# Decay attention into two mixture layers on one core: first weight halves loaded ahead of the third unit, mixture steps ordered behind earlier scores

## The chip, the cores and the metric

One core of one Trainium2 chip runs the whole program in one launch. The metric is device time in microseconds (us), start to end of the launch. The median of three runs before the change is 562.1 us (561.58 to 562.75).

## The reference

Three stages follow each other; each reads what the one before it wrote.

```python
# 1. attention with decay, b over blocks of 64 positions, 2 batches x 8 heads, head size 64
intra = (q_b k_b^T * Dmask) v_b
inter = (q_b * lam**(pos+1)) kv_state
out_b = intra + inter
kv_state = lam**block * kv_state + (k_b * lam**(block-1-pos))^T v_b
# 2. first mixture layer on the 1536 x 512 rows
h = x @ w_in            # 512 x 2048, given as 64-bit floats
x2 = (h * cos(h)) @ w_out
# 3. second mixture layer: each row goes to one of 8 experts
e = argmax(x2 @ w_gate)
y = relu(x2[e] @ w1[e]) @ w2[e] * softmax_weight * sigmoid(x2 @ w_output_gate)[e]
```

## The kernel before

**Attention** is cut into 12 units u0 to u11 of 128 positions (6 chunks x 2 batches, the batches in turn). A unit has three parts, and the loop over `i` at the end of the program issues part 1 of unit i, part 2 of unit i-1 and part 3 of unit i-2. Part 1 (`a_s1`) turns the keys and the queries on TensorE (tiles tkT and tqT, in two PSUM buffers), ACT copies them to SBUF as kT and qT, DVE multiplies the turned queries by powers of lambda (qw), and POOL scales the keys (kd). Part 2 (`a_s2`) makes the scores sc on TensorE, and DVE multiplies them by the decay (pt). Part 3 (`a_s3`) makes the new state sn on TensorE, in one of the same two PSUM buffers as tkT and tqT, then the output o in one PSUM buffer, from qw and the state st and from pt and the values; DVE folds sn into st; ACT and DVE split o into two parts xs (a rounded part and the rest) for the next layer.

**Weights of the first mixture layer** come as 64-bit floats, half by half (128 x 512 numbers, 512 KB). `w_load` asks for the next half on the SP queue into a buffer raw; `w_split` converts it: ACT takes the high words (x, L207), DVE does three operations on x (L208, L209, L211), ACT rounds the result into the weight tile (w_in or w_out, L219), POOL subtracts and writes the rest (L220). x has two buffers. The constant SPLITS says in which round `i` halves are converted: one in each of rounds 2 to 5, two in rounds 6 and 7. The first step needs four halves of w_in: two for each of the first two weight pieces, of which the first piece alone is needed by step 0.

**Mixture steps** B(j, p) multiply 256 rows (block j) by weight piece p: 24 matmuls h of 256 columns (L443), a cosine chain on ACT and DVE (L472 to L478), 12 matmuls acc of 512 columns (L455), which come two steps later. Six such steps (NSA) are issued inside the attention loop, one in each round from START = 6 on, the rest behind it.

**What sets the order.** The kernel is written without hand-placed waits. A scheduler takes the instructions as the program issues them and fixes an order for each engine; every engine then runs its own list strictly in that order, and semaphores between engines are put in by the framework. `tc.issue_after(ins)` makes the scheduler place every instruction of the block that runs on the engine of `ins` behind `ins`.

**The end.** `finish` scales the result of an expert's tile (ACT for the first 128 rows, DVE for the second), and an indirect DMA from POOL scatters the rows to the output.

Of the kernel before, what the change touches and what calls it, by code (L numbers as in the profile page):

```python
# [8 lines left out]
F32 = mybir.dt.float32  # L9
F32R = mybir.dt.float32r  # L10
BF16 = mybir.dt.bfloat16
I32 = mybir.dt.int32
AF = mybir.ActivationFunctionType
ALU = mybir.AluOpType
# [14 lines left out]
def kernel(  # L29
# [93 lines left out]


    HP = 2
    steps = [("B", j, p) for j in range(FIRST) for p in range(HP)]
    NSA = len(steps)
    steps += [("B", j, p) for p in range(NP) for j in range(FIRST, NB)]
# [56 lines left out]
    def w_split():  # L185
        i = nxt["split"]
        if i >= len(order):
            return
        nxt["split"] += 1
        key = order[i]  # L190
        r = raw_t.pop(key)
        if key[0] in ("w1", "w2"):
            t = w_tile(key[0] == "w1", place(*key), "w_" + "_".join(str(z) for z in key))
            nc.scalar.copy(out=t[:, 0, :], in_=r)  # L194
            nc.vector.tensor_sub(out=t[:, 1, :], in0=r, in1=t[:, 0, :].bitcast(F32))  # L195
            wt[key] = t
        else:
            name, p, f = key
            if f == 0:
                wt[name, p] = w_tile(name == "in", p, f"w_{name}_{p}")  # L200
            t = wt[name, p]
            words = r.rearrange("p (n t) -> p n t", t=2)
            low, high = words[:, :, 0], words[:, :, 1]
            x = cv_p.tile([128, ROW], I32, tag="x", name="x")[:, 0:512]


            nc.scalar.activation(out=x.bitcast(F32), in_=high.bitcast(F32), func=AF.Copy, scale=F64_SCALE)  # L207
            nc.vector.tensor_scalar(x, x, 3, None, ALU.logical_shift_left)  # L208
            nc.vector.scalar_tensor_tensor(  # L209
                out=x, in0=low, scalar=29, in1=x, op0=ALU.logical_shift_right, op1=ALU.bitwise_or)  # L210
            nc.vector.scalar_tensor_tensor(  # L211
                out=x, in0=high, scalar=-0x80000000, in1=x, op0=ALU.bitwise_and, op1=ALU.bitwise_or)
            xf = x.bitcast(F32)
            if name == "in":
                xf = xf.rearrange("p (k f) -> p k f", k=KD)
                hi, lo = [t[:, s].rearrange("p (k f) -> p k f", k=KD)[:, :, f * 128:(f + 1) * 128] for s in range(2)]
            else:
                hi, lo = [t[:, s, f * 512:(f + 1) * 512] for s in range(2)]
            nc.scalar.copy(out=hi, in_=xf)  # L219
            nc.gpsimd.tensor_sub(out=lo, in0=xf, in1=hi.bitcast(F32))  # L220
        w_load()
# [4 lines left out]
    def wB(key, s, f):  # L226
# [8 lines left out]
        tc.tile_pool(name="at2", bufs=2),  # L235
        tc.tile_pool(name="at3", bufs=3),
        tc.tile_pool(name="raw2", bufs=2),
    ]
    qk_p, v_p, at2, at3, pools["raw2"] = [c.__enter__() for c in at_cms]
    ps_cms = [  # L240
        tc.tile_pool(name="ps_tr", bufs=2, space=PSUM),
        tc.tile_pool(name="ps_sc", bufs=2, space=PSUM),
# [57 lines left out]
    def setup_late():  # L300
        nc.gpsimd.memset(ones, 1.0)
        nc.gpsimd.memset(upper, 1.0)
        nc.gpsimd.affine_select(
            out=upper, in_=upper, compare_op=ALU.is_gt, fill=0.0, base=0,
            pattern=[[1, 128]], channel_multiplier=-1)
        nc.gpsimd.memset(accoh, 0.0)
        nc.gpsimd.memset(skip, 0.0)
        nc.gpsimd.iota(lane, pattern=[[0, 1]], base=CAP, channel_multiplier=1, allow_small_or_imprecise_dtypes=True)
        for e in range(E):
            nc.gpsimd.memset(iota8[:, :, e:e + 1], float(e - E))  # L310
            nc.gpsimd.memset(eoff[:, :, e:e + 1], float(e * CAP))
        nc.gpsimd.iota(tid, pattern=[[CH, NCH], [S, B]], base=0, channel_multiplier=1)
        nc.gpsimd.memset(wgs, 0.0)
        for w, o in ((w_gate, 0), (w_og, E)):
            nc.sync.dma_start(out=wgs[:, :, o:o + E], in_=w.rearrange("(k p) e -> p k e", p=128))

# [4 lines left out]
    def xs_tile(slot, name="xs"):  # L321
        return xs_p.tile([128, 2, KD, TB], F32R, tag=f"xs{slot}", name=name)

    kT_t, qT_t, qw_t, kd_t, p_t = {}, {}, {}, {}, {}

    def turned(src, pool, name):
        ps = ps_tr.tile([128, PR, 128], F32, tag="tr", name="t" + name)
# [21 lines left out]
    def a_s2(u):  # L349
        if u < 0 or u >= NU:  # L350
            return
        kT = kT_t.pop(u)
        qb = qT_t.pop(u)
        pt = at2.tile([128, H, CH], F32, tag="pt", name="pt")

        sc = [ps_sc.tile([128, PR, CH], F32, tag="sc", name="sc") for _ in range(2)]
        for pr in range(PR):
            for t in range(2):
                to = slice(64 * t, 64 * t + 64)
                nc.tensor.matmul(sc[t][:, pr, :], lhsT=kT[to, pr, :], rhs=qb[to, pr, :], start=True, stop=True)  # L360
        for t in range(2):
            nc.vector.tensor_mul(out=pt[:, t::2, :], in0=sc[t], in1=dec[:, t::2, :])
        p_t[u] = pt

    def a_s3(u):
# [5 lines left out]
        if c + 1 < NCH:  # L371
            kd = kd_t.pop(u)
            sn = ps_tr.tile([128, PR, 64], F32, tag="tr", name="sn")
            for h in range(H):
                sl = slice(64 * (h % 2), 64 * (h % 2) + 64)
                nc.tensor.matmul(  # L376
                    sn[sl, h // 2, :], lhsT=kd[:, h, :], rhs=vs[:, h, :], start=True, stop=True)
        o = ps_o.tile([128, PR, 128], F32, tag="o", name="o")
        if c > 0:
            qw = qw_t.pop(u)  # L380
            for pr in range(PR):
# [254 lines left out]

    rows, scl = {}, {}

    def finish(acc, t, s, who):
        y = tmp_p.tile([128, DM], F32, tag="a", name="y")  # L640
        if t == 0:
            nc.scalar.activation(out=y, in_=acc, func=AF.Copy, scale=s[:, t:t + 1])  # L642
        else:
            nc.vector.tensor_scalar(y, acc, s[:, t:t + 1], None, ALU.mult)
        put = nc.gpsimd.indirect_dma_start(  # L645
            out=out, out_offset=bass.IndirectOffsetOnAxis(ap=who, axis=0),
            in_=y, in_offset=None, bounds_check=NT - 1, oob_is_err=False)
        apart(put, puts)
# [165 lines left out]
    def second(i):  # L814
# [4 lines left out]
        if ph == "B":  # L819
# [3 lines left out]
                half_evac(j, acc_t.pop(j))  # L823
            if p == NP - 1:
                r_evac(j, acc_t.pop(j))
                parts = [(r_tr, (j,), 0), (r_mm, (j,), 2), (r_arg, (j,), 1), (r_rank, (j,), 3)]
                if j == EARLY:
                    parts += [(h_rows, (0,), 0), (r_skip, (), 2)]
                if j == FIRST - 1:
                    parts.append((routed, (), 0))  # L830
                if j == EARLY:
                    w_load()
                rout.append({"since": 0, "parts": parts})
            if j == (NB if p < HP else FIRST) - 1:
                del wt["out", p]
        elif ph == "H":
# [9 lines left out]
        else:  # L846
# [10 lines left out]
            if p == EP - 1:  # L857
                acc_t.pop(j)
                s, who = scl.pop(j)
                for z in range(2):  # L860
                    finish(accs[z], z, s, who[:, z, :])

    todo = 0

# [37 lines left out]
            h_prep(1, 1)  # L902

    SPLITS = [0, 0, 1, 1, 1, 1, 2, 2]
    START = 6
    for i in range(NU + 2):
        a_load(i + 2)
        if i == 0:
            for _ in range(4):
                w_load()  # L910
        a_s1(i)
        if i == 0:
            setup_late()
        a_s2(i - 1)
        if i == 1:
            setup_powers()
# [1 line left out]
        for _ in range(SPLITS[i] if i < len(SPLITS) else 0):  # L918
            w_split()
        if START <= i < START + NSA:  # L920
            step(i - START)
        if i >= 9 and i % 2:
            b_split(FIRST + (i - 9) // 2)

    for c in reversed(at_cms):
        c.__exit__(None, None, None)
    del pools["raw2"]
    pools["att"].__exit__(None, None, None)
    seconds(NSA)
    for c in reversed(ps_cms):  # L930
# [124 lines left out]
```

## Time and profile before

| what | value |
|---|---|
| median of 3 runs | 562.1 us |
| the profiled execution | 562.26 us |
| its span, first to last instruction | 560.4 us |
| TensorE (PE) busy | 539.1 us, 96% |
| DVE, ACT, POOL busy | 339.0, 306.2, 101.5 us |
| HBM read and written | 67.31 and 18.24 MB |

The profile gives times within the span; 1.86 us of the profiled execution lie outside it. A matmul's end is modelled, so that two that follow each other overlap in the rows; the start of the next one tells what a group took. PEld is the weight load in front of a matmul. "Idle before" is the time that an engine stood still in front of an instruction, with the instruction that ended it.

### The profile page before, as it was taken

The numbers are of one execution on the slowest core, as the hardware profiler recorded it, in microseconds if no ns is written. First come the engines' busy times: TensorE is split into PE (matmuls) and PEld (weight loads), VectorE is DVE, ScalarE is ACT, GpSimd is POOL, SyncE is SP. The second block draws the span as 40 slices with busy tenths as digits, with TensorE's granted clock in tenths as the row PEclk, the third lists the DMA queues.
The fourth block names the chain that finished last, engine by engine and source line by source line (L and its number), as shares of the span: only waits on it lengthen the run. The fifth ranks groups of instructions, "written<-read, shape, count | busy, mean of one in ns | idle before, by whom it ended". The sixth has DMA issues, their size and how long they took to land.

```text
span 560.4 us, 9916 instructions
## 1 busy us (share of the span) xinstructions
PE 539.1 (96%) x3940; PEld 479.3 (86%) x3940; DVE 339.0 (60%) x604; ACT 306.2 (55%) x492; POOL 101.5 (18%) x129
## 2 busy tenths in 40 slices
PE   8699999999999999999999989999999999999993
PEld 7578888889898999988898969799999999999982
DVE  4787647587878764345564569734677764855110
ACT  3455546477776765554554597625766654643110
POOL 4443400223222230001111200211011101101011
PEclk9999999999999999999999999999999999999997
DMA  8999841044533374201262345851688975740000
GB/s 196 258 262 282 228 133 39 10 142 151 187 114 113 113 280 145 76 39 40 66 203 79 91 139 190 258 198 55 196 287 292 296 246 183 252 156 25 1 26 34
DMA packets 84296, 85.24 MB, mean 152 GB/s; under 512 B 41486, under 2 KB 66062, under 8 KB 83472
## 3 DMA queue, kind: packets, MB, share of 16 engines
q1 hardware_dynamic: 82000, 78.09, 45.4%
q0 software_dynamic: 2240, 6.42, 2.9%
q8 instruction: 33, 0.54, 0.4%
q14 instruction: 23, 0.19, 0.1%
HBM read 67.31 MB, written 18.24 MB: 153 GB/s over the span
## 4 chain that ended last, share of the span: by engine, by line
PE 57%; issue 23%; DMA 9%; DVE 4%; POOL 3%; ACT 2%; SPq 0%; POOLq 0%; DVEq 0%; ACTq 0%
PE h L443 20%; PE acc L455 20%; DMA out_dram<-y,who 4%; PE hh L712 4%; PE acc L733 2%; DMA raw<-in_moe_w_dram 2%; PE sc L360 2%; POOL out_dram L645 2%; PE o L389 2%; PE o L384 2%; DMA xs_d<-xrow,si 2%; PE tqT L329 1%; PE sn L376 1%; DVE w_w L195 1%; DMA q<-in_q_dram 1%
## 5 line engine op out<-in xcount | busy, mean ns | idle before, releaser
L455 PE MATMUL acc<-w_out,g 128*128 128x512 f32 x576 | 141.5, 394 | 0.3 <-ACT g L477 0.3
L455 PEld LDWEIGHTS acc<-w_out,g 128*128 128x128 f32 x576 | 104.8, 188 | 21.5 <-issue 1.2
L443 PE MATMUL h<-xs,w_in 128*128 128x256 f32 x720 | 93.1, 284 | 3.7 <-POOL w_in L220 2.6
L443 PEld LDWEIGHTS h<-xs,w_in 128*128 128x128 f32 x720 | 89.4, 190 | 7.4 <-POOL w_in L220 3.0
L195 DVE TENSOR_TENSOR w_w<-raw,w_w 128x1024 fp32r<-128x1024 f32 x64 | 76.9, 1222 | 25.3 <-ACT w_w L194 25.1
L194 ACT CAST w_w<-raw 128x1024 fp32r<-128x1024 f32 x64 | 65.7, 1048 | 33.4 <-DMA raw<-in_moe_w_dram 27.0
L443 PEld LDWEIGHTS h<-xs,w_w 128*128 128x128 f32 x576 | 72.0, 191 | 1.9
L443 PE MATMUL h<-xs,w_w 128*128 128x256 f32 x576 | 72.6, 282 | 0.0
L455 PE MATMUL acc<-w_w,g 128*128 128x512 f32 x288 | 69.9, 393 | 0.0
L474 DVE SCALAR_TENSOR_TENSOR a<-a,t 128x512 f32<-128x512 f32 x48 | 36.0, 750 | 46.7 <-ACT a L473 46.7
L455 PEld LDWEIGHTS acc<-w_w,g 128*128 128x128 f32 x288 | 52.6, 188 | 10.1
L443 PE MATMUL h<-xback,w_in 128*128 128x256 f32 x432 | 55.5, 283 | 0.0
L443 PEld LDWEIGHTS h<-xback,w_in 128*128 128x128 f32 x432 | 52.8, 189 | 1.7 <-issue 1.2
L472 ACT ACTIVATE t<-h,quarter 128x512 f32<-128x512 f32 x48 | 32.9, 686 | 35.4 <-PE h L443 35.2
L645 POOL DMA_INDIRECT out_dram<-y,who x16 | 19.1, 1195 | 162.4 <-ACT y L642 146.5
L477 ACT CAST g<-a 128x512 fp32r<-128x512 f32 x48 | 29.7, 619 | 28.1 <-DVE a L476 28.0
L476 DVE TENSOR_TENSOR a<-t,h 128x512 f32<-128x512 f32 x48 | 32.9, 684 | 16.9 <-ACT t L475 16.0
L475 ACT ACTIVATE t<-a 128x512 f32<-128x512 f32 x48 | 30.3, 631 | 18.5 <-DVE a L474 18.4
L478 DVE TENSOR_TENSOR g<-a,g 128x512 fp32r<-128x512 f32 x48 | 33.9, 707 | 10.1 <-ACT g L477 9.3
L473 ACT ACTIVATE a<-t,magic 128x512 f32<-128x512 f32 x48 | 34.8, 724 | 1.1
L599 POOL DMA_INDIRECT xs_d<-xrow,si x12 | 15.1, 1261 | 101.0 <-DVE si L597 73.9
L702 DVE SCALAR_TENSOR_TENSOR g<-h,g 128x512 fp32r<-128x512 f32 x24 | 16.5, 687 | 25.7 <-ACT g L701 25.6
(144 smaller groups left out, 632.4 us busy)
## 6 DMA issues: line engine op xcount, KB each, us to landing
raw<-in_moe_w_dram SPq DMA_DIRECT2D x64, 512.0 KB, 4.7
raw<-in_moe_w_in_dram SPq DMA_DIRECT2D x16, 512.0 KB, 3.9
raw<-in_moe_w_out_dram SPq DMA_DIRECT2D x16, 512.0 KB, 3.6
xs_d<-zrow SPq DMA_DIRECT2D x16, 266.0 KB, 3.9
x_d<-xrow SPq DMA_DIRECT2D x6, 532.0 KB, 2.9
rows<-xs_d SPq DMA_DIRECT2D x6, 532.0 KB, 4.5
k<-in_k_dram SPq DMA_DIRECT2D x12, 256.0 KB, 4.9
q<-in_q_dram SPq DMA_DIRECT2D x12, 256.0 KB, 4.9
```

The costliest lines, as they stand in the source:

```text
L194: nc.scalar.copy(out=t[:, 0, :], in_=r)
L195: nc.vector.tensor_sub(out=t[:, 1, :], in0=r, in1=t[:, 0, :].bitcast(F32))
L443: nc.tensor.matmul(h[:, f * n:(f + 1) * n], lhsT=wA(key, ws, kk, f), rhs=x[:, xx, kk, :], start=(z == 0), stop=(z == 3 * KD - 1))
L455: nc.tensor.matmul(accs[t], lhsT=g[:, gs, f, t * 128:(t + 1) * 128], rhs=wB(key, ws, f), start=(first and n == 0), stop=(last and n == 5))
L472: head = nc.scalar.activation(out=t, in_=h, func=AF.Identity, bias=quarter, scale=INV2PI / WIDE)
L473: heads.append((head.ins, nc.scalar.activation(out=a, in_=t, func=AF.Identity, bias=magic).ins))
L474: nc.vector.scalar_tensor_tensor(out=a, in0=a, scalar=MAGIC, in1=t, op0=ALU.subtract, op1=ALU.subtract)
L475: nc.scalar.activation(out=t, in_=a, func=AF.Sin, scale=-TWOPI)
L476: nc.vector.tensor_mul(out=a, in0=t, in1=h)
L477: nc.scalar.copy(out=g[:, 0].rearrange("p f t -> p (f t)"), in_=a)
L478: nc.vector.tensor_sub(out=g[:, 1].rearrange("p f t -> p (f t)"), in0=a, in1=g[:, 0].rearrange("p f t -> p (f t)").bitcast(F32))
L645: put = nc.gpsimd.indirect_dma_start(out=out, out_offset=bass.IndirectOffsetOnAxis(ap=who, axis=0), in_=y, in_offset=None, bounds_check=NT ...
```

## The change

Seven edits, five of them in the attention loop:

1. In round 0 two halves of w_in are asked for ahead of the loads of unit u2, and two behind it; before, all four behind it.
2. A pool cv2 of two more buffers holds x of every second half while the attention runs.
3. The outputs o of u1 and u2 go to the PSUM pool of acc; the others stay in the one buffer of ps_o.
4. The loads of the two gate matrices (16 KB each) move from round 0 to round NU = 12, the start of the end of the loop.
5. Each step in the attention loop is placed behind the last score matmul of unit i-3: step 0 behind the scores of u3.
6. In the last expert's second tile, `finish` gives half of the columns to ACT and half to DVE.
7. The routing jobs count their delay from the turn in which they are put down, with delay 1 for the first part in place of 0, except for the last of them.

```diff
-            x = cv_p.tile([128, ROW], I32, tag="x", name="x")[:, 0:512]
+            x = (pools["cv2"] if "cv2" in pools and i % 2 else cv_p).tile([128, ROW], I32, tag="x", name="x")[:, 0:512]
...
+        tc.tile_pool(name="cv2", bufs=2),
...
+    def setup_gates():
         for w, o in ((w_gate, 0), (w_og, E)):
             nc.sync.dma_start(out=wgs[:, :, o:o + E], in_=w.rearrange("(k p) e -> p k e", p=128))
...
-                nc.tensor.matmul(sc[t][:, pr, :], lhsT=kT[to, pr, :], rhs=qb[to, pr, :], start=True, stop=True)
+                scored[u] = nc.tensor.matmul(
+                    sc[t][:, pr, :], lhsT=kT[to, pr, :], rhs=qb[to, pr, :], start=True, stop=True)
...
-        o = ps_o.tile([128, PR, 128], F32, tag="o", name="o")
+        early = u + 2 < START and u % 3
+        o = (pools["acc"] if early else ps_o).tile([128, PR, 128], F32, tag="acc" if early else "o", name="o")
...
-    def finish(acc, t, s, who):
+    def finish(acc, t, s, who, last=False):
...
+        elif last:
+            half = DM // 2
+            nc.scalar.activation(out=y[:, 0:half], in_=acc[:, 0:half], func=AF.Copy, scale=s[:, t:t + 1])
+            nc.vector.tensor_scalar(y[:, half:], acc[:, half:], s[:, t:t + 1], None, ALU.mult)
...
-                parts = [(r_tr, (j,), 0), (r_mm, (j,), 2), (r_arg, (j,), 1), (r_rank, (j,), 3)]
+                parts = [(r_tr, (j,), 0 if j == FIRST - 1 else 1), (r_mm, (j,), 2), (r_arg, (j,), 1), (r_rank, (j,), 3)]
...
-                rout.append({"since": 0, "parts": parts})
+                rout.append({"since": clock[0], "parts": parts})
...
     for i in range(NU + 2):
+        if i == 0:
+            for _ in range(2):
+                w_load()
         a_load(i + 2)
         if i == 0:
-            for _ in range(4):
+            for _ in range(2):
                 w_load()
         a_s1(i)
         if i == 0:
             setup_late()
+        if i == NU:
+            setup_gates()
...
         if START <= i < START + NSA:
-            step(i - START)
+            with tc.issue_after(scored[i - 3].ins):
+                step(i - START)
```

What the scheduler makes of it, at three places. The line numbers of the change are its own: L396 was L389 (o from pt), L391 was L384 (o from qw and the state), L364 was L360 (scores), L381 was L376 (sn), L333 was L329 (turning), L450 was L443 (h).

TensorE, from the scores of u2 to those of u3, before; w_in_344 is the first weight piece, st_174 the state of the first batch:

```order
L360 MATMUL sc<-qT,kT 128x128 x8
L389 MATMUL o<-pt,v 64x128 x8
L384 MATMUL o<-qw,st_174 64x128 x8
L389 MATMUL o<-pt,v 64x128 x8
L443 MATMUL h<-xs,w_in_344 128x256 x20
L329 MATMUL tkT<-ident,k 128x128 x4
L443 MATMUL h<-xs,w_in_344 128x256 x4
L329 MATMUL tqT<-ident,q 128x128 x4
L376 MATMUL sn<-v,kd 64x64 x8
L360 MATMUL sc<-qT,kT 128x128 x8
```

TensorE, the same stretch and on to the first h, now:

```order
L364 MATMUL sc<-qT,kT 128x128 x8
L391 MATMUL o<-qw,st_177 64x128 x8
L396 MATMUL o<-pt,v 64x128 x8
L333 MATMUL tkT<-ident,k 128x128 x4
L333 MATMUL tqT<-ident,q 128x128 x4
L381 MATMUL sn<-v,kd 64x64 x8
L364 MATMUL sc<-qT,kT 128x128 x8
L333 MATMUL tkT<-ident,k 128x128 x4
L391 MATMUL o<-qw,st_178 64x128 x7
```

The 24 matmuls h of step 0 stood between the output of u2 and the scores of u3; now they stand behind the output of u3. The outputs of u0 and u1 have both moved ahead of the turning of u2.

DVE, from the decay of u0 and u1 to the first state of the second batch, now (L209, L210, L212 are the three operations on x, L416 the rest of xs, L347 qw, L405 the first state, L367 pt):

```order
L367 TENSOR_TENSOR pt<-sc,dec 128x4x128 x4
L209 TENSOR_SCALAR x<-x 128x512
L210 SCALAR_TENSOR_TENSOR x<-raw,x 128x512
L416 TENSOR_TENSOR xs<-o,xs 128x4x128
L212 SCALAR_TENSOR_TENSOR x<-raw,x 128x512
L416 TENSOR_TENSOR xs<-o,xs 128x4x128
L209 TENSOR_SCALAR x<-x 128x512
L210 SCALAR_TENSOR_TENSOR x<-raw,x 128x512
L212 SCALAR_TENSOR_TENSOR x<-raw,x 128x512
L347 TENSOR_TENSOR qw<-tqT,lpow 128x512
L405 COPY st_177<-sn 128x256
L367 TENSOR_TENSOR pt<-sc,dec 128x4x128 x2
```

Two halves are converted ahead of qw, of the first state and of the decay of u2; before, these three stood ahead of the first half. The third and fourth half follow directly behind them, ahead of the state of the second batch, as before.

ACT, around the turned keys and queries of u3 (the second pair of COPY rows here), now:

```order
L335 COPY kT<-tkT 128x512
L220 CAST w_in_345<-x 128x4x128
L335 COPY qT<-tqT 128x512
L220 CAST w_in_345<-x 128x4x128
L208 ACTIVATE x<-raw 128x512 x2
L415 CAST xs<-o 128x4x128
L220 CAST w_in_490<-x 128x4x128
L335 COPY kT<-tkT 128x512
L220 CAST w_in_490<-x 128x4x128
L335 COPY qT<-tqT 128x512
```

The copy of the keys of u3 stands behind the rounding of the third half, that of its queries behind the rounding of the fourth; before, the fourth stood behind both copies.

## Rows read from the trace of the kernel before

**Rows 1.** The page, busy time of each engine, share of the span, instructions.
```profile
PE 539.1 (96%) x3940; PEld 479.3 (86%) x3940; DVE 339.0 (60%) x604; ACT 306.2 (55%) x492; POOL 101.5 (18%) x129
```

**Rows 2.** Busy us by engine in stretches; then PE clock (1.00 full), DMA share, GB/s.
```profile
16.00:30.00 14.00, 9.16 (x112) 7.66 (x110) 11.71 (x18) 6.91 (x13) 7.18 (x5) 1.00 0.99 254
36.00:105.00 69.00, 69.00 (x743) 57.43 (x738) 44.87 (x73) 35.73 (x60) 14.79 (x16) 1.00 0.58 161
551.00:554.00 3.00, 0.06 (x1) 0.00 (x0) 0.75 (x1) 0.00 (x0) 0.97 (x1) 1.00 0.32 115
556.00:560.00 4.00, 0.00 (x0) 0.00 (x0) 0.00 (x0) 0.00 (x0) 0.10 (x1) 0.50 0.01 2
```

**Rows 3.** Timeline of TensorE: start, us, what, idle before and what ended it.
```profile
19.65 1.09 PE L384 MATMUL o<-qw,st 64*64 64x128 f32 x16 [1.76 <-DVE xs L409]
...
26.47 0.98 PE L443 MATMUL h<-xs,w_in 128*128 128x256 f32 x6 [1.30 <-POOL w_in L220]
...
29.63 1.16 PE L360 MATMUL sc<-qT,kT 64*128 64x128 f32 x16 [0.21 <-ACT qT L331]
31.57 0.43 PE L384 MATMUL o<-qw,st 64*64 64x128 f32 x2 [0.78 <-DVE qw L343]
...
33.78 0.43 PE L389 MATMUL o<-pt,v 128*64 128x128 f32 x2 [0.19 <-DVE pt L362]
```

**Rows 4.** Chain of waits in order of time: the 24 matmuls h of one step.
```profile
108.31 2.84 PE h L443 x24
```

**Rows 5.** Timeline of DVE, the first conversions.
```profile
12.98 1.29 DVE L362 TENSOR_TENSOR pt<-sc,dec 128x512 f32<-128x512 f32 x2 [2.02 <-PE sc L360]
...
17.85 0.42 DVE L208 TENSOR_SCALAR x<-x 128x512 int32<-128x512 int32 x1
18.31 0.69 DVE L209 SCALAR_TENSOR_TENSOR x<-raw,x 128x512 int32<-128x512 int32 x1
18.91 0.68 DVE L409 TENSOR_TENSOR xs<-o,xs 128x512 fp32r<-128x512 f32 x1
...
28.21 1.65 DVE L209 SCALAR_TENSOR_TENSOR x<-raw,x 128x512 int32<-128x512 int32 x1
```

**Rows 6.** Timeline of POOL, the same stretch.
```profile
11.09 1.06 POOL L346 TENSOR_TENSOR kd<-k,dec 128x512 f32<-128x512 f32 x1 [0.35 <-DMA k<-in_k_dram]
...
27.85 1.46 POOL L220 TENSOR_TENSOR w_in<-x,w_in 128x512 fp32r<-128x512 f32 x1
31.31 1.27 POOL L220 TENSOR_TENSOR w_in<-x,w_in 128x512 fp32r<-128x512 f32 x1 [2.00 <-ACT w_in L219]
```

**Rows 7.** Timeline of ACT, the same stretch.
```profile
24.01 0.61 ACT L219 CAST w_in<-x 128x512 fp32r<-128x512 f32 x1
...
28.99 0.59 ACT L331 COPY qT<-tqT 128x512 f32<-128x512 f32 x1
```

**Rows 8.** Groups by line, 0 to 120 us: busy us, mean ns, idle before.
```profile
L268 PEld LDWEIGHTS up<-zz 128*128 128x128 f32 x24 | 4.6, 300 | 1.1 <-DVE quarter L283 1.1
...
L329 PEld LDWEIGHTS tkT<-ident,k 128*128 128x128 f32 x48 | 5.4, 141 | 1.2 <-ACT kT L331 0.5 <-issue 0.2 <-DVE pt L362 0.2
...
L209 DVE SCALAR_TENSOR_TENSOR x<-raw,x 128x512 int32<-128x512 int32 x13 | 10.3, 795 | 0.3
L211 DVE SCALAR_TENSOR_TENSOR x<-raw,x 128x512 int32<-128x512 int32 x12 | 9.0, 752 | 0.2
L208 DVE TENSOR_SCALAR x<-x 128x512 int32<-128x512 int32 x13 | 7.8, 603 | 3.0 <-ACT x L207 3.0
...
L396 DVE TENSOR_TENSOR st<-st,sn 128x256 f32<-128x256 f32 x8 | 3.3, 417 | 8.4 <-PE sn L376 8.4
```

**Rows 9.** Who waited for whom, SP's own queue, 60 to 120 us.
```profile
SPq L178 <- DVE x L211: 45.0, 4, 21.3
```

**Rows 10.** Timeline of the tail.
```profile
551.10 0.75 DVE L644 TENSOR_SCALAR y<-acc,sm 128x512 f32<-128x512 f32 x1 [6.87 <-PE acc L455]
552.12 0.97 POOL L645 DMA_INDIRECT out_dram<-y,who  x1 [1.76 <-DVE y L644]
```

More of the change, by code (lines that the diff above doesn't have):

```diff
@@ L125 @@
     HP = 2
+    START = 6
     steps = [("B", j, p) for j in range(FIRST) for p in range(HP)]
@@ L237 @@
         tc.tile_pool(name="raw2", bufs=2),
+        tc.tile_pool(name="cv2", bufs=2),
     ]
-    qk_p, v_p, at2, at3, pools["raw2"] = [c.__enter__() for c in at_cms]
+    qk_p, v_p, at2, at3, pools["raw2"], pools["cv2"] = [c.__enter__() for c in at_cms]
     ps_cms = [
@@ L322, in xs_tile @@
         return xs_p.tile([128, 2, KD, TB], F32R, tag=f"xs{slot}", name=name)
-    kT_t, qT_t, qw_t, kd_t, p_t = {}, {}, {}, {}, {}
+    kT_t, qT_t, qw_t, kd_t, p_t, scored = {}, {}, {}, {}, {}, {}
     def turned(src, pool, name):
@@ L860, in second @@
                 for z in range(2):
-                    finish(accs[z], z, s, who[:, z, :])
+                    finish(accs[z], z, s, who[:, z, :], j == E - 1)
     todo = 0
@@ L904 @@
     SPLITS = [0, 0, 1, 1, 1, 1, 2, 2]
-    START = 6
     for i in range(NU + 2):
+        if i == 0:
+            for _ in range(2):
+                w_load()
         a_load(i + 2)
         if i == 0:
-            for _ in range(4):
+            for _ in range(2):
                 w_load()
@@ L926 @@
         c.__exit__(None, None, None)
-    del pools["raw2"]
+    del pools["raw2"], pools["cv2"]
     pools["att"].__exit__(None, None, None)
```

## The prediction

> **What bounds the kernel now.** The page first: TensorE is busy for 539.1 of 560.4 us [rows 1], so the time can fall only where it stands still or by less work. The windows say where that is: from 36 to 105 us it has no idle time at all, while between 16 and 30 us it is busy for 9.16 of 14 us, and DVE for 11.71 [rows 2]. So what is gained or lost ahead of about 36 us reaches the end of the program one to one, as long as the order behind it stays full. The timeline of TensorE names the waits of that stretch: 1.76 us in front of the output of u2, 1.30 us in a step that wants a converted weight half (one of two such), 0.78 and 0.19 us behind the scores of u3 [rows 3]. Each is ended by DVE or by POOL, which hands over what DVE converted. DVE is thus the second bound of this stretch, and the question is whether the new order gets more out of it.
>
> What the reader should see in the rows of DVE and POOL is that the two get in each other's way. An operation on x takes 0.69 us alone, but 1.65 us at 28.21: it ends at 29.86, 0.55 us after the POOL subtraction that runs from 27.85 to 29.31 [rows 5, 6]. That subtraction takes 1.27 us where nothing meets it, 1.46 us here [rows 6].
>
> **The change part by part.** The large term is edit 5: step 0 no longer fills the stretch ahead of the scores of u3. Before, these started at 29.63 [rows 3], with all 24 matmuls h of step 0 done. A step's 24 matmuls take 2.84 us [rows 4]. In the new order they come behind the output of u3, so the scores of u3 must start before 29.63 - 2.84 = 26.8 us to be level on that count alone. When they start follows from the lists of DVE, POOL and ACT, which I work through in us.
>
> - The scores of u0 and u1 need what they needed before. They are no longer cut by the turning of u2 and end near 11.7, so the decay of u1 takes DVE from 11.9 to 13.1; it started at 12.98 before [rows 5].
> - DVE goes on with the first half: 0.46 us from the first operation to the second and 0.60 to the next one [rows 5], then xs of u0 (0.61), 14.8. The third operation meets kd of u2 on POOL. Its keys landed at 11.09 before [rows 6]; two halves more ahead of them, 1 MB at 254 to 290 GB/s (the first is of [rows 2], the second is my allowance for larger pieces), are 3.6 to 4.1 us, of which u2's own queue hides some: about 14.1. So kd holds POOL from 14.1 to 15.2, and DVE ends at 15.8; xs of u1 to 16.4.
> - Second half: first operation to 16.85. ACT has rounded the first half by 16.5 (0.61, [rows 7]), and POOL's subtraction of 1.27 us stands in front of the second operation until 18.1, which ends 0.55 us behind it, 18.65; third 19.35; qw and the first state to 20.3. The output of u2 starts there. The buffer that it waited for until 19.65 is free long before (edit 3), but this wait of 1.76 us has only changed its owner.
> - The decay of u2 to 21.5; third half: 0.46, 0.60, and the third operation finds POOL busy with the second half's subtraction, the scaling of the state and kd of u3 (1.06 us, [rows 6]) until 24.0: it ends at 24.5. xs of u2 to 25.1.
> - ACT rounds the third half from 24.6 to 25.2 and only then copies the keys of u3, to 25.8. Both PSUM buffers of the turning are held, so sn of u1 waits for this copy from about 23.1: 2.6 us idle.
> - Fourth half: 0.46 us to 25.6; the subtraction of the third half (25.3 to 26.6) stands in front of the second operation, 27.1; third 27.8; ACT rounds to 28.4 and copies the queries of u3 in 0.59 us [rows 7]: the scores of u3 start at **28.9**.
>
> That is 28.9 + 2.84 - 29.63 = **+2.1 us**. Behind the scores of u3 the waits of 0.78 and 0.19 us [rows 3] go, since no step competes for DVE there; a step's h that waits for its one PSUM buffer may come back with some 0.4 us (my allowance between nothing and the 1.30 us of [rows 3]). Net **-0.6 us**, between -1.0 and +0.3.
>
> *The mean prices or the single rows?* Over 13 halves the three operations take 603, 795 and 752 ns on average [rows 8]. With these means the same chain reaches the scores of u3 at 26.4, and with the single rows, in which an operation stands until POOL is done, at 28.9. I take 28.9, because the lists say which operations meet: in four places a subtraction, a state or a kd is due just ahead of an operation on x. By the page SBUF — State Buffer of the Trainium skill (who interferes with whom), a DVE operation with two SBUF inputs and a POOL operation that reads SBUF exclude each other for the whole instruction; by that rule the sum is the one with 28.9, and the row of 1.65 us agrees with it.
>
> **The smaller edits.** Edit 2 frees the third half from waiting for x; the chain above has that in it. Edit 1 brings weights earlier than DVE can take them up, and u2 later by some 3 us; the chain has both. Edit 4 takes two small loads out of a stretch in which the DMA share is 0.99 [rows 2]: u3 lands earlier, but the turning of u3 starts at 22.3, later than it could. At its new place SP waits up to 21.3 us for a raw buffer anyway [rows 9], so two more issues there cost nothing; without that cover it would be a few us on a queue that nobody waits for. The first step's h and its chain start later by 11 us, but acc follows two steps behind it, and TensorE has attention work in between. Edit 7 lets each first part run at the next turn, as before: no term. Edit 6 halves the last DVE operation, 0.75 us in front of the last scatter [rows 10]; a DVE operation of 256 columns out of PSUM takes 0.417 us [rows 8], and ACT's half runs beside it: **-0.3 us**, between -0.35 and nothing.
>
> **Sum:** 2.1 - 0.6 - 0.3 = **+1.2 us**. The profiled execution took 562.26 us, so it would be 563.5; the median stands 0.16 us lower, so I forecast **563.3 us**. The likeliest case has its own range of 562.3 to 564.3: the start of the scores of u3 can be off by 0.7, the net behind it by as much.
>
> **Rivals.**
> - *The collisions don't happen as I place them* (the other side). Were POOL's subtractions to fall into gaps of DVE, the prices would be the means, and the scores of u3 would start at 26.4: 26.4 + 2.84 - 29.63 - 0.6 - 0.3 = -1.3, **560.8 us**. It decides at 29.63 - 2.84 + 0.6 + 0.3 = 27.7: a start of u3's scores before that makes the kernel faster. For it: kd and the subtractions move a little with each landing. Against it: the four meetings follow from the order of the lists and not from a landing. Chance 0.15.
> - *TensorE's clock falls.* Between 22.3 and 28.9 us TensorE would have only the turning of u3 and sn of u1, under 2 us of work. Before, the granted clock stayed at 1.00 from 16 to 30 us with 9.16 us of work; at the end of the program it is still 1.00 at 551 to 554 us and 0.50, the level of 1.2 GHz, from 556 us on, with the last matmul ended near 551 [rows 2]. If it falls ahead of u3's scores, the matmuls up to its rise take twice as long. The first 24 matmul records of the program show such a price: weight loads of 300 ns against 141 later, over 4.6 us [rows 8], so some 2.4 us lost: **565.7 us**. Against it: the longest single wait that I place is 2.6 us, and waits of 1.76 us left the clock alone. Chance 0.15.
> - *The owed matmuls come back cheaper.* The order has 8 rows fewer on TensorE, thus fewer changes between matmuls of different shape. If each change costs 0.15 us, 1.2 us return: **562.1 us**, no change. Against it: five of the eight rows that went stood ahead of u3's scores, where TensorE waits anyway. Chance 0.15.
>
> **How the numbers follow.** The forecast has 0.55. A measurement tells about 0.2% from no change, 1.1 us here. The likeliest case lies just above that line, so it splits: 0.28 slower, 0.27 within. With the clock's 0.15 and little of the rest, slower gets 0.43; within 0.2% gets 0.27 + 0.13 = 0.40; faster gets 0.17, nearly all of it from the first rival. The range of 561.0 to 565.7 leaves out the better half of that rival and a tail above the clock's case.
>
> **What would show it.** Right: the 24 matmuls h behind the output of u3; its scores at 28 to 30 us, in front of them waits of over 2 us ended by ACT's copies of kT and qT; operations on x of 1.1 us and more beside POOL's subtractions; no wait for xs in front of the output of u2; a last DVE operation near 0.4 us. Wrong: scores of u3 before 27.7 us, a granted clock below 1.00 ahead of 36 us, or new idle time of TensorE between 36 and 105 us.

## The result and the profile after

The changed kernel takes 565.99 us (median of 5 runs, 565.03 to 566.48), the kernel before on the same chip 562.10 (561.58 to 562.75): a ratio of **1.0059, 95% interval 1.0044 to 1.0075**. By the medians (1.0069) it is slower by 3.9 us, by the ratio by 3.3, where the forecast was +1.2. The profiled execution is the one of 565.99 us; its span is 564.2 us (560.4 before).

The windows of the changed kernel, to be held against [rows 2] (stretch, length, busy us and instructions of PE, PEld, DVE, ACT and POOL, granted clock, DMA share, GB/s):

```profile
16.00:22.00 6.00, 3.44 (x48) 2.97 (x47) 5.90 (x10) 2.86 (x5) 2.61 (x2) 0.80 1.05 285
22.00:26.00 4.00, 4.00 (x28) 3.14 (x24) 2.66 (x4) 1.68 (x3) 2.70 (x3) 0.50 1.05 236
26.00:30.00 4.00, 1.28 (x21) 1.14 (x22) 3.10 (x5) 1.10 (x2) 1.54 (x2) 0.93 0.98 266
30.00:36.00 6.00, 6.00 (x61) 4.69 (x60) 2.32 (x5) 1.74 (x3) 1.85 (x3) 0.73 1.02 246
36.00:60.00 24.00, 24.00 (x288) 20.31 (x286) 18.26 (x32) 13.18 (x22) 9.60 (x11) 1.00 0.91 252
60.00:105.00 45.00, 44.80 (x446) 37.61 (x446) 28.28 (x44) 23.15 (x37) 4.70 (x6) 1.00 0.37 107
```

The granted clock was 1.00 in all of these before. Now it is 0.50, the level of 1.2 GHz, through 22 to 26 us, and between the two levels on either side; with 0.5 for the lower one, the four means make 2.4 + 4.0 + 0.6 + 3.2 = 10.2 us at half speed. A busy PE between 22 and 26 us is thus not more work but the same at half speed. Behind 36 us hardly anything new stands idle: 0.20 us.

The timeline of TensorE, against [rows 3] (start, duration, engine, line, operation, out<-in, count, idle time before and what ended it):

```profile
15.89 0.69 PE L381 MATMUL sn<-v,kd 128*64 128x64 f32 x16
17.16 1.16 PE L364 MATMUL sc<-qT,kT 64*128 64x128 f32 x16 [0.59 <-ACT qT L335]
20.29 1.97 PE L391 MATMUL o<-qw,st 64*64 64x128 f32 x16 [1.97 <-DVE st L405]
22.19 1.97 PE L396 MATMUL o<-pt,v 128*64 128x128 f32 x16
...
26.03 0.83 PE L381 MATMUL sn<-v,kd 128*64 128x64 f32 x16
29.58 1.92 PE L364 MATMUL sc<-qT,kT 64*128 64x128 f32 x16 [2.72 <-ACT qT L335]
31.44 1.11 PE L333 MATMUL tkT<-ident,k 128*128 128x128 f32 x4
32.48 1.42 PE L391 MATMUL o<-qw,st 64*64 64x128 f32 x14
...
35.76 1.16 PE L364 MATMUL sc<-qT,kT 64*128 64x128 f32 x16
...
37.87 1.20 PE L450 MATMUL h<-xs,w_in 128*128 128x256 f32 x8
```

The scores of u3 start at 29.58 us, forecast 28.9, and the h of step 0 come behind the output of u3, at 37.87. The output of u2 takes 1.97 us for each of its two parts where it took 1.09 (the first is in [rows 3] at 19.65); the scores of u3 take 1.92 instead of 1.16. Those are the half-speed matmuls.

DVE in the same stretch, against [rows 5]:

```profile
14.91 1.06 DVE L212 SCALAR_TENSOR_TENSOR x<-raw,x 128x512 int32<-128x512 int32 x1
...
16.94 1.64 DVE L210 SCALAR_TENSOR_TENSOR x<-raw,x 128x512 int32<-128x512 int32 x1
18.61 0.69 DVE L212 SCALAR_TENSOR_TENSOR x<-raw,x 128x512 int32<-128x512 int32 x1
...
22.52 0.99 DVE L212 SCALAR_TENSOR_TENSOR x<-raw,x 128x512 int32<-128x512 int32 x1
24.83 0.69 DVE L416 TENSOR_TENSOR xs<-o,xs 128x512 fp32r<-128x512 f32 x1 [1.31 <-ACT xs L415]
25.43 1.51 DVE L209 TENSOR_SCALAR x<-x 128x512 int32<-128x512 int32 x1
```

and POOL, against [rows 6]:

```profile
14.36 1.06 POOL L350 TENSOR_TENSOR kd<-k,dec 128x512 f32<-128x512 f32 x1 [3.71 <-DMA k<-in_k_dram]
16.70 1.33 POOL L221 TENSOR_TENSOR w_in<-x,w_in 128x512 fp32r<-128x512 f32 x1 [1.28 <-ACT w_in L220]
...
25.39 1.27 POOL L221 TENSOR_TENSOR w_in<-x,w_in 128x512 fp32r<-128x512 f32 x1 [0.95 <-ACT w_in L220]
```

The reader is to see the pairs: POOL's subtraction ends at 18.03 and DVE's operation at 18.58; POOL's at 26.66 and DVE's at 26.94. The first two of the four collisions are where the forecast put them: beside kd of u2 (14.91) and beside the first subtraction (16.94). The other two moved. The third operation of the third half was to stand until 24.5 and ended at 23.51; behind it DVE waits 1.31 us for ACT's xs of u2, which the half-speed output of u2 made late. Of the fourth half it is the first operation that stands beside POOL's subtraction (25.43, 1.51 us in place of 0.42), not the second.

The tail, against [rows 10], one row of each engine that takes part (ACT's half of y, DVE's half, the scatter):

```profile
554.59 0.47 ACT L652 ACTIVATE y<-acc,sm 128x256 f32<-128x256 f32 x1 [1.98 <-PE acc L462]
```

```profile
555.10 0.48 DVE L653 TENSOR_SCALAR y<-acc,sm 128x256 f32<-128x256 f32 x1 [7.37 <-ACT y L652]
```

```profile
555.86 0.97 POOL L656 DMA_INDIRECT out_dram<-y,who  x1 [2.00 <-DVE y L653]
```

The halves don't run beside each other: DVE's starts 0.04 us after ACT's has ended, released by it. From the start of y to the scatter it is 1.27 us; before, 552.12 - 551.10 = 1.02 [rows 10].

### The profile page after: what moved, and what is told of

The parts are those of the page before. It is cut to its first block, busy times and chain, and to the rows that moved or that the text cites. A ratio compares the mean times of both kernels' runs of the same rounds, so it can differ in the third digit from the quotient of the medians.

```text
span 564.2 us, 9929 instructions
## 1 busy us (share of the span) xinstructions
PE 543.0 (96%) x3940; PEld 483.5 (86%) x3940; DVE 339.3 (60%) x604; ACT 306.6 (54%) x493; POOL 99.6 (18%) x129
## 4 chain that ended last, share of the span: by engine, by line
PE 58%; issue 23%; DMA 8%; DVE 5%; ACT 3%; POOL 3%; POOLq 0%; SPq 0%; ACTq 0%
PE h L450 21%; PE acc L462 20%; DMA out_dram<-y,who 4%; PE hh L723 4%; PE acc L744 2%; PE sc L364 2%; DMA raw<-in_moe_w_dram 2%; PE o L391 2%; POOL out_dram L656 2%; PE o L396 2%; DMA xs_d<-xrow,si 2%; DVE w_w L196 1%; PE up L270 1%; PE tkT L333 1%; PE sn L381 1%
## 5 line engine op out<-in xcount | busy, mean ns | idle before, releaser
L450 PE MATMUL h<-xs,w_in 128*128 128x256 f32 x720 | 92.0, 283 | 1.3 <-DVE a L483 1.3
L450 PEld LDWEIGHTS h<-xs,w_in 128*128 128x128 f32 x720 | 89.1, 190 | 4.8 <-DVE a L483 1.9
L450 PEld LDWEIGHTS h<-xs,w_w 128*128 128x128 f32 x576 | 72.0, 191 | 1.9
L450 PE MATMUL h<-xs,w_w 128*128 128x256 f32 x576 | 72.6, 282 | 0.0
L450 PE MATMUL h<-xback,w_in 128*128 128x256 f32 x432 | 55.5, 283 | 0.0
L450 PEld LDWEIGHTS h<-xback,w_in 128*128 128x128 f32 x432 | 52.8, 189 | 1.7 <-issue 1.2
L713 DVE SCALAR_TENSOR_TENSOR g<-h,g 128x512 fp32r<-128x512 f32 x24 | 16.5, 687 | 25.2 <-ACT g L712 24.9
```

Source lines behind the costliest of these rows:

```text
L450: nc.tensor.matmul(h[:, f * n:(f + 1) * n], lhsT=wA(key, ws, kk, f), rhs=x[:, xx, kk, :], start=(z == 0), stop=(z == 3 * KD - 1))
```

## The experiments

To compare traces I use one **mark** behind the attention: the start of the first ACT operation on the h of step 6, whose matmuls no longer depend on anything ahead of 36 us. Before, it is

```profile
111.18 0.69 ACT L472 ACTIVATE t<-h,quarter 128x512 f32<-128x512 f32 x1 [3.32 <-PE h L443]
```

and in the changed kernel

```profile
114.66 0.69 ACT L479 ACTIVATE t<-h,quarter 128x512 f32<-128x512 f32 x1 [3.30 <-PE h L450]
```

The first scores start between 8.1 and 9.2 us, as the first transfers land, so the table takes the mark from the start of the first score matmul (8.48 us before, 8.52 in the changed kernel) and gives its difference to the kernel before.

| kernel | scores of u3 at | half-speed stretches ahead of 40 us | mark, us against before | ratio to before |
|---|---|---|---|---|
| changed kernel | 29.58 | 20 to 26, 30 to 33 us | +3.44 | 1.0059 |
| e1, e9: three gaps kept busy | 29.72, 29.26 | none, none | +1.46, +1.52 | 1.0041, 1.0019 |
| e2: without edit 5 | 29.33 | none | -0.63 | 0.9990 |
| e3: edit 5 alone | 29.70 | 26 to 37 us | +3.50 | 1.0052 |
| e4: without edit 6 | 29.83 | 20 to 27, 30 to 34 us | +3.46 | one run |
| e5: first gap kept busy | 28.95 | 26 to 33 us | +3.12 | one run |
| e6: four subtractions on DVE | 26.43 | 28 to 35 us | +1.57 | one run |
| e7: e6 without edits 5, 6 | 26.95 | 30 to 33 us | -0.51 | 0.9939 |
| e8: without edits 4, 5, 6 | 30.80 | 23 to 26 us | -0.66 | 1.0007 |
| e10: e7 with two subtractions on DVE | 26.86 | none | -4.26 | 0.9942 |
| e11: before, four subtractions on DVE | 28.36 | none | -3.06 | 0.9933 |

**e1, the gaps kept busy.** Is it the clock? The edit adds matmuls on zeros and holds the order:

```diff
+IDLE = {'o2': 8, 'sn1': 9, 'sc3': 10}
...
+            kept[place] = [
+                nc.tensor.matmul(t[:, 0:CH], lhsT=zz, rhs=zz, start=True, stop=True).ins for _ in range(count)]
...
+    pin()
```

`pin` holds the instructions of the attention in the changed kernel's order on every engine, and puts the added ones in front of the place that each key names (o2 is the output of u2).

> The changed kernel, every engine's instructions in the same order, with 27 extra 128x128 matmuls on the array of zeros written into the still unused buffer of h: 8 ahead of the output of u2, 9 ahead of sn of u1, 10 ahead of the scores of u3, where TensorE stands idle. The numbers of the output do not depend on them. Theory A (the clock): the idle stretch let the clock fall, and the half-speed matmuls are what the forecast of +1.2 us lacked. With the array kept busy the granted clock is 1.00 from 10 to 60 us, the scores of u3 start near 29.1 (29.58 in the changed kernel), and the time is 563.3 to 564.2 us, some 2.3 us below the changed kernel. Theory B (waits and the owed step alone): the stretch waits for DVE, POOL and ACT anyway, so half-speed matmuls are hidden and the time stays at 565.5 to 566.5 us even at a granted clock of 1.00.

Measured: 565.52 us, ratio 1.0041 (1.0025 to 1.0057), the mark 2.0 us earlier than in the changed kernel, the clock at 1.00 up to 330 us. There this execution has a fall of its own, where TensorE stands idle 1.5 of 30 us (its windows; same columns as above):

```profile
300.00:330.00 30.00, 28.50 (x189) 24.68 (x187) 14.96 (x43) 17.39 (x26) 3.38 (x8) 1.00 0.29 91
330.00:335.00 5.00, 4.34 (x24) 4.35 (x25) 3.32 (x9) 4.69 (x9) 0.00 (x0) 0.66 0.58 180
```

The mark speaks for the clock. The time does not decide: in us it is at the lower edge of theory B's range, but the kernel before stands at 562.72 us in these runs, 0.6 higher, and by the ratio it lies between the two theories; the profiled execution also lost time at 330 us. So the experiment was done again.

**e9, the same without edit 6.**

> The kernel with all three gaps kept busy once more, without edit 6, to take the price of the clock a second time: its first profile had the clock at 1.00 to 330 us and one fall there. Theory A: the granted clock is 1.00 from 10 to 60 us, the first ACT operation on h of step 6 begins at 112.6 to 113.2 us (111.18 before, 114.66 in the changed kernel), and the time is 0.1 to 0.4% above the kernel before, as the order alone costs some 1.5 us. Theory B (half speed is hidden behind the waits): the mark lies at 114.2 or later and the time 0.5% or more above.

Measured: 564.21 us, ratio 1.0019 (1.0006 to 1.0033), the interval wholly below the changed kernel's. Its windows:

```profile
16.00:22.00 6.00, 5.37 (x71) 4.59 (x70) 5.93 (x10) 3.05 (x6) 2.67 (x3) 1.00 0.97 262
22.00:26.00 4.00, 4.00 (x42) 3.72 (x40) 3.90 (x6) 1.70 (x3) 2.72 (x3) 1.00 1.02 231
26.00:30.00 4.00, 3.86 (x49) 3.60 (x50) 3.06 (x4) 1.11 (x2) 1.99 (x2) 1.00 1.06 278
30.00:36.00 6.00, 6.00 (x81) 4.67 (x79) 3.24 (x6) 1.75 (x3) 2.73 (x4) 1.00 0.89 224
```

and of its timeline of TensorE (keep is the added work; L400 is the line of the scores here, L431 that of the output from the state)

```profile
20.77 1.09 PE L431 MATMUL o<-qw,st 64*64 64x128 f32 x16
...
26.63 2.50 PE L346 MATMUL keep<-zz 128*128 128x128 f32 x20
29.26 1.16 PE L400 MATMUL sc<-qT,kT 64*128 64x128 f32 x16
...
33.88 1.16 PE L400 MATMUL sc<-qT,kT 64*128 64x128 f32 x16
```

and the mark (L521 and L492 are its lines here):

```profile
112.36 0.69 ACT L521 ACTIVATE t<-h,quarter 128x512 f32<-128x512 f32 x1 [3.30 <-PE h L492]
```

The mark itself, 112.36 us, is 0.24 us earlier than the range given for theory A; the first scores, at 8.14, are 0.38 us earlier than in the changed kernel.

What follows: the clock costs 3.44 - 1.52 = 1.9 us at the mark and the order alone 1.5, and theory B falls. The split depends on where the count begins, for the keys of u2 landed later in e1 and e9: their kd of u2 starts 6.54 and 6.70 us behind the first scores, that of the changed kernel 5.84 (14.36 - 8.52). The output of u2 comes 5.93 us behind that kd in all three. Counted from the output of u2 on, the mark comes after 94.37 us in the changed kernel and after 91.69 and 91.59 in e1 and e9: so counted, the clock costs 2.7 to 2.8 us and the order alone 0.7.

Where these 2.7 to 2.8 us arise is in the same rows. From the output of u2 to the scores of u3 it is 8.49 us in e1, e5 and e9, and 9.29 in the changed kernel (9.30 in e4, its order with the same fall): 0.80 us, since the half-speed output of u2 holds up ACT's and DVE's lists. From the scores of u3 to those of u4 it is 4.62 us here and 6.18 there: 1.56 us, paid in full. The last 0.3 to 0.4 us come behind the scores of u4, near 60 us.

**e5, the first gap alone kept busy.**

```diff
-IDLE = {'o2': 8, 'sn1': 9, 'sc3': 10}
+IDLE = {'o2': 8}
```

> The changed kernel with the order of every engine held as it is, and 8 extra matmuls on zeros in the first gap alone, ahead of the output of u2. As a mark, the first ACT operation on the h of step 6 began at 111.18 us before, at 114.66 in the changed kernel and at 112.92 with all three gaps kept busy. If the fall belongs to the first gap alone, the clock now stays at 1.00 through 36 us and the mark lies at 112.7 to 113.2. If the later waits ahead of sn of u1 and of the scores of u3 (2.3 and 2.5 us at full clock) lower it too, the granted clock falls between 24 and 30 us, and the mark lies at 113.8 to 115.

Measured: 565.5 us (one run), the mark at 114.17. Its windows:

```profile
22.00:26.00 4.00, 2.06 (x30) 1.68 (x28) 3.93 (x5) 1.69 (x3) 2.72 (x3) 1.00 0.99 223
26.00:30.00 4.00, 1.64 (x24) 1.46 (x21) 2.76 (x4) 1.10 (x2) 2.00 (x3) 0.50 1.04 262
```

```profile
25.71 0.88 PE L419 MATMUL sn<-v,kd 128*64 128x64 f32 x16 [1.94 <-ACT kT L371]
28.95 2.08 PE L400 MATMUL sc<-qT,kT 64*128 64x128 f32 x16 [2.36 <-ACT qT L371]
```

The later waits lower the clock by themselves, and 1.6 of the 1.9 us stay (2.0 to 2.1 of the 2.7 to 2.8, counted from the output of u2). This is the stretch that the forecast named; at full clock the wait of sn of u1 for ACT's copy, which the changed kernel hides behind half-speed work, is there too.

**e2 and e3, edit 5 taken out and put in alone.** e2 replaces the block of edit 5 by `step(i - START)`; e3 is the kernel before with

```diff
-            step(i - START)
+            with tc.issue_after(scored[i - 3].ins):
+                step(i - START)
```

> The changed kernel without edit 5: step 0 is issued where the order puts it, ahead of the scores of u3; edits 1 to 4, 6 and 7 stay. Theory A (edit 5 is the cause: the owed 24 matmuls and the idle stretch it leaves): the time falls to 560 to 561.5 us, below the kernel before, with the granted clock at 1.00 from 10 to 36 us. Theory C (edits 1 to 3 thin out the work of TensorE between 16 and 20 us, ahead of the output of u2, and the clock falls there whatever edit 5 does): the granted clock is again 0.5 from 19 or 20 us on, and the time is 562.5 to 564 us.

> The kernel before with edit 5 alone. Theory A: everything up to 21.7 us stays as before, then step 0 waits behind the scores of u3; these still start near 29.5, since DVE's list hardly changes, so the 24 matmuls are owed in full: +2.5 us by the order, and with no work for TensorE between 23 and 28 us the clock falls there as well, some 2 us more: 566 to 567.5 us. Theory C: the clock falls only where edits 1 to 3 thin out the work, so it stays at 1.00 here and the time is 564 to 565 us.

Measured: e2 562.43 us, ratio 0.9990 (0.9977 to 1.0004); e3 565.98 us, ratio 1.0052 (1.0034 to 1.0070). In e2's profile the clock stays at 1.00 to the end of the attention, though the same wait stands in front of the output of u2:

```profile
17.33 0.50 PE L450 MATMUL h<-xs,w_in 128*128 128x256 f32 x2 [0.17 <-ACT w_in L220]
17.81 1.16 PE L364 MATMUL sc<-qT,kT 64*128 64x128 f32 x16
20.95 1.09 PE L391 MATMUL o<-qw,st 64*64 64x128 f32 x16 [1.98 <-DVE st L405]
```

This execution has the highest mean granted clock of the twelve runs of e2, 0.996; the lowest has 0.989, so others may have had a fall. In e3, without edits 1 to 3, the fall is later and the loss at the mark the same:

```profile
28.65 1.12 PE L378 MATMUL sn<-v,kd 128*64 128x64 f32 x16 [3.96 <-ACT kT L332]
29.70 2.08 PE L361 MATMUL sc<-qT,kT 64*128 64x128 f32 x16
```

```profile
30.00:36.00 6.00, 5.83 (x41) 4.54 (x40) 3.06 (x6) 1.20 (x2) 2.62 (x3) 0.50 1.04 254
```

Here theory C had 1.00, so it is not the cause of the loss, though e8 below shows that the clock can fall without edit 5 as well. The time of e3 alone would not tell: 565.98 us is just under theory A's 566, and its ratio on 562.10 us gives 565.0, the top of theory C's range.

Edit 5 carries the loss: alone it gives +3.50 at the mark, all seven edits +3.44, and all but edit 5 -0.63. The size expected of e2 was missed: the wait of 1.98 us stays and another of 1.27 us stands ahead of the scores of u3, so it gains too little for its time to be told from no change.

**e4, without edit 6.** The last finish is one DVE operation again.

```diff
-        elif last:
-            half = DM // 2
-            nc.scalar.activation(out=y[:, 0:half], in_=acc[:, 0:half], func=AF.Copy, scale=s[:, t:t + 1])
-            nc.vector.tensor_scalar(y[:, half:], acc[:, half:], s[:, t:t + 1], None, ALU.mult)
```

> The changed kernel with the last finish as before: one DVE operation of 512 columns. The trace of the changed kernel has DVE's half starting 0.04 us after ACT's half ends. Theory A (the two halves read one bank of PSUM and are put one after the other): from the end of the last matmul to the end of y 0.79 us as before, against 0.99 us in the changed kernel: the end comes 0.2 to 0.3 us earlier. Theory B (ACT was merely ahead, and one half after the other costs no more than the whole): no difference between the two tails.

```profile
554.67 0.75 DVE L651 TENSOR_SCALAR y<-acc,sm 128x512 f32<-128x512 f32 x1 [6.86 <-PE acc L462]
```

```profile
555.70 0.97 POOL L652 DMA_INDIRECT out_dram<-y,who  x1 [1.76 <-DVE y L651]
```

1.03 us from y to the scatter in place of 1.27: edit 6 costs 0.24 us. That both halves read one PSUM bank is the likely reason for the wait, but not a shown one: they also write one tile y, and neither halves in two banks nor two tiles were tried. By the page PSUM — Partial Sum Buffer of the Trainium skill (PSUM bank collisions raise a hardware error), two engines have to be kept apart by bank and quadrant even when both only read; the rows are in line with it, with the 0.04 us between the halves.

**e6, the first four subtractions on DVE.** Do the collisions carry the chain?

```diff
-            nc.gpsimd.tensor_sub(out=lo, in0=xf, in1=hi.bitcast(F32))
+            (nc.vector if i < 4 else nc.gpsimd).tensor_sub(out=lo, in0=xf, in1=hi.bitcast(F32))
```

> The changed kernel with the subtraction of the first four weight halves on DVE (4 more operations of 0.7 us each there) in place of POOL (1.3 us each). Theory A (an operation on x stands until POOL's subtraction is done): the four collisions go, and with 2.8 us more work on DVE the scores of u3 still start earlier, at 26.9 to 28.2 us instead of 29.58. Theory D (the prices are means and POOL's work does not hold DVE up): DVE's list grows by 2.8 us and the scores of u3 start at 30.5 to 32.5.

```profile
17.88 0.68 DVE L210 SCALAR_TENSOR_TENSOR x<-raw,x 128x512 int32<-128x512 int32 x1
...
22.50 1.54 DVE L210 SCALAR_TENSOR_TENSOR x<-raw,x 128x512 int32<-128x512 int32 x1
```

The scores of u3 start at 26.43, 3.15 us earlier and ahead of theory A's 26.9, with four operations more on DVE. Counted from the first scores, and against e1 and e9, which like this one had the clock at 1.00 up to there, it is 3.0 and 3.2 us (17.96 in place of 20.96 and 21.12). The operation that took 1.64 us takes 0.68; what still takes over 1.4 us (22.50, and two more) meets kd on POOL, which ran from 22.28 to 23.49. Theory D falls. The clock fell here too, at 28 us, and took part of it back.

**e7, e10 and e11, towards a faster kernel.** e7 is e6 without edits 5 and 6, e10 the same with `i < 2`, e11 the kernel before with e6's edit alone.

> The changed kernel without edits 5 and 6 and with the first four subtractions on DVE. Theory A: step 0 fills the waits again, the collisions are gone and the tail is the old one: 1 to 3 us below the kernel before, 559.5 to 561.5 us, the scores of u3 near 26.5 to 28. Theory D: the longer list of DVE costs what step 0 brings, and the time is 562 to 564 us.

> The changed kernel without edits 5 and 6, with the subtraction of the first two weight halves on DVE and of all others on POOL. With four of them on DVE the output of u3 waited 1.45 us for DVE, and the time was 559.42 us where the kernel before had 563.03. Theory A (DVE's list is the bound, and POOL's subtraction costs only where it meets an operation on x): two subtractions fewer on DVE take that wait away, the scores of u3 stay near 26.5 us, and the time is 0.5 to 1 us lower still, a ratio to the kernel before of 0.989 to 0.994. Rival: the subtractions of the third and fourth half, on POOL again, meet DVE's operations of the second pair and give the gain back: 0.995 to 0.998.

> The kernel before with nothing changed but the first four subtractions on DVE: what of the gain belongs to the collisions alone, without edits 1 to 4 and 7. Theory A (collisions are the bound of the stretch ahead of 30 us): the scores of u3, at 29.63 before, start at 28.4 to 29.2, the waits behind them shrink as well, and the time is 0.3 to 0.6% below the kernel before. Theory E (edits 1 to 3 are needed, since without them the third half waits for a buffer of x and the output of u2 for a buffer of o): less than 0.2%.

Measured: e7 559.42 us, ratio 0.9939 (0.9915 to 0.9963); e10 559.05, 0.9942 (0.9924 to 0.9960); e11 559.24, 0.9933 (0.9918 to 0.9948). All three beat both kernels by more than the bound of 0.2%. e11 stands beside the rows of before [rows 3]: the wait of 1.30 us for POOL's w_in is gone, the other is 0.67 us, and the scores of u3 start 1.3 us earlier; time and scores are a little better than theory A gave.

```profile
24.43 0.51 PE L443 MATMUL h<-xs,w_in 128*128 128x256 f32 x2 [0.67 <-ACT w_in L219]
...
28.36 1.16 PE L360 MATMUL sc<-qT,kT 64*128 64x128 f32 x16 [0.57 <-ACT qT L331]
```

So one line on the kernel before does what seven edits did not, and theory E falls. At the mark e10 is 1.2 us ahead of e11; the times don't tell them apart. The further gain expected of e10 over e7 did not come in the time either (0.9942 against 0.9939), though its scores of u4 come at 31.92 without a wait of TensorE for DVE; the marks of the two don't compare, as the trace of e7, of its longest run, has a fall of the clock.

**e8, without edits 4, 5 and 6.**

> The changed kernel without edits 4, 5 and 6 (the two small gate loads back at the start, step 0 ahead of the scores of u3, the last finish whole). Theory A: edits 1 to 3 alone gain some 0.6 us by the mark of step 6 (110.55 in the kernel without edit 5, 111.18 before), the tail 0.25 on that kernel: 561 to 562.2 us on this chip, where the kernel before is at 562.7 or the like; the gate loads change under 0.5 us either way. Rival: the gate loads, back ahead of the keys of u3, make the turning of u3 late, and the time is 562.7 us or more.

Measured: 563.68 us, ratio 1.0007 (0.9986 to 1.0028). By its number the rival came true, but the trace doesn't show its reason at work: the scores of u3 are late, at 30.80, and the clock falls, though no step is held back here, and yet the mark stands at -0.66, as in e2. The trace is of a run of 561.03 us, the second shortest of twelve (559.36 to 566.81), and what makes the others longer isn't in it.

```profile
22.00:26.00 4.00, 4.00 (x26) 3.34 (x25) 3.25 (x7) 1.10 (x2) 1.07 (x3) 0.61 1.13 256
```

What the gate loads cost by themselves stays open.

## Why the prediction was right, and where it was wrong

The direction was right (slower, the most likely of the three). The time came 2.7 us above the forecast, at the upper end of the range, 565.7: by the medians 0.3 us above it, by the ratio (562.10 x 1.0059 = 565.4) 0.3 below. Point by point:

- **The chain up to the scores of u3**: right in its steps. The output of u2 was placed at 20.3 and came at 20.29; the second half's operations were to end at 18.65 and 19.35 and ended at 18.58 and 19.30; no wait for xs is left in front of the output of u2. From there to the scores of u3 it placed 8.6 us, and at full clock (e1, e5, e9) it is 8.49; the 29.58 of the changed kernel has 0.80 us of half speed in it. One step of the working is off by 0.3 us: a subtraction of 1.27 us from 16.5 on ends at 17.8, not 18.1 (it ran from 16.70 to 18.03).
- **The owed step** (+2.1) **and the waits behind it** (-0.6): the sum of +1.5 is what e1 and e9 measured at the mark, +1.46 and +1.52, but that is luck, for the parts missed in opposite ways. In e1 and e9 the later keys put the scores of u3 20.96 and 21.12 us behind the first scores, where the forecast's 28.9 means 20.4, so the first term was +2.7 and +2.8. From those scores to the mark it took 83.20 and 83.10 us, before 81.55, of which 2.84 are step 0: the second term was -1.2 and -1.3. With the keys as early as in the changed kernel the two make 0.7. That waits behind the scores of u3 go is in the rows: none stands between 29.58 and 37.87.
- **The single rows instead of the mean prices**: right, and e6 shows the cause, at the same clock 3.0 to 3.2 us. Of the four meetings two moved in the changed kernel, behind the half-speed output of u2. The rival without collisions (560.8) is out.
- **The clock**: this rival, with a chance of 0.15, is what happened, on top of the forecast, and with it came one of the forecast's own signs of being wrong, a granted clock below 1.00 ahead of 36 us. The step that failed is the reason against it, that waits of 1.76 us had left the clock alone and the longest one placed was 2.6 us: in the changed kernel the clock fell while TensorE waited 1.97 us, after a wait of 0.59 us and a single group of scores between them, and ahead of the stretch that the forecast named (22.3 to 28.9 us). A wait was judged alone, and not the stretch around it with step 0 taken out.
- **What half speed costs** was put at 2.4 us and measured 1.9 at the mark, 2.7 to 2.8 from the output of u2 on. That it fits is luck, since the price was read from the start of the program, where weight loads took 300 ns [rows 8] and the granted clock is 1.00, as this window of the kernel before shows:

```profile
3.00:5.00 2.00, 2.00 (x11) 2.00 (x11) 0.64 (x3) 0.00 (x0) 0.22 (x2) 1.00 0.88 193
```

- **Half speed in the changed kernel**: at a granted clock of 0.50, from 22 to 26 us of the changed kernel, the weight loads of the turned keys and queries took 217 and 230 ns, against 141. The windows show 10.2 us at half speed, and the loss was below 3 us, because part of that stretch was waiting for DVE and ACT. The page TensorE: Matmul & The Clock Gate of the Trainium skill (Terms) prices half speed at the time spent there times one half; an estimate by it is 5.1 us, and here the measurement decides.
- **Edit 6** (-0.3): wrong. It cost 0.24 us. The step took ACT's half as running beside DVE's; it runs in front of it.
- **Fewer changes of shape** (562.1): not shown. The part behind the scores of u3 gave back about 0.6 us more than the forecast had, and no run tells whether by waits or by this.

Sum at the mark: 1.5 + 1.9 + 0.24 = 3.6 us (with the other split 0.7 + 2.7 + 0.24), against 3.8 in the spans, 3.9 in the medians and 3.3 by the ratio. So the direction came for the reason forecast only in part: the order was to cost 1.2 us, and more than half of the loss is the clock.

## What to carry to other kernels

A step that fills waits can also keep TensorE's clock up; before it is moved out of a thin stretch, price that stretch at half speed, and count the matmuls behind its last wait (1.56 us here) and those whose result the awaited engines take up (0.80 us). Where DVE is the bound and POOL works beside it, compare one DVE operation's duration with and without a POOL operation over it: here four subtractions moved from POOL to DVE made DVE's list longer and the kernel 0.67% faster. Splitting an operation over two engines gained nothing here, where both halves read one PSUM tile and write one tile: look at when the second half starts.

## What was not expected of the hardware

- The clock can fall in this stretch without edit 5: the trace of e8 shows it at 23 us. Its 12 runs had mean granted clocks from 0.984 to 0.995 over the span, with 566.81 us at the lowest and 559.36 at the highest; where in the program the other runs lost clock is not on record.
- Two executions had a fall in the middle of a program that had run at 1.00 so far: e1 (0.66 from 330 to 335 us, shown above) and e11 (0.66 from 325 to 330 us). The ACT operations on h behind it stood 1.5 us later against the kernel before than those ahead of it, in both.
- In e6 DVE was busy for all of the 6.00 us from 16 to 22 us (5.90 in the changed kernel) and still handed over sooner, with more operations to do: here the duration of a DVE operation says as much of POOL's list as of its own size. Even the operation on x with one input, 0.42 us alone, took 1.51 us beside POOL's subtraction (25.43 in the rows above).
